# Triangular inverses of large batches on VectorE alone, in row order, with norms from lanes, fix-ups on ScalarE, and a replanned instruction order

## The chip, the cores and the metric

The kernel runs on one core of a Trainium2 chip (TensorE, VectorE, ScalarE, GpSimd, the SyncE DMA queue). The metric is device time in microseconds, the median of the runs: 554.67 us (554.18 to 555.22, three runs).

## What is computed

A delta-rule attention over 768 positions for 16 heads of width 48, followed by two mixture-of-experts layers (8 experts each, top-1). Cut to the part that matters here:

```python
k_n = k / (norm(k) + 1e-06)
for t in range(S):
    y[:, :, t] = q[:, :, t] @ state
    v_old = state^T k_n[:, :, t]
    state = state + beta_t * outer(k_n[:, :, t], v[:, :, t] - v_old)
x = y as [1536, 384]; x = moe(x); out = moe2(x)     # route to argmax expert, relu(x w1) w2, gate
```

## The kernel before

**Tiling.** The 768 positions are cut into 24 chunks of 32. Inside a chunk the recurrence is a triangular system: with the Gram matrix of the chunk's keys, a 32x32 unit triangle is inverted for each of the 16 heads, and the state then moves from chunk to chunk by matrix products. Six groups q of four chunks share their loads.

**Gram matrices.** `gram(q)` multiplies keys with keys and queries on TensorE (L504); ScalarE evicts them to `Gs` (L515) and `PT` (L520); GpSimd masks `PT` (`affine_select`, L550).

**Inverses in lanes.** `inlane(bi, pri)` takes a batch of chunks (`BATCH` = 4, 4, 8, 8 chunks; batches 0 and 1 with `BLK` 1, batches 2 and 3 with `BLK` 0). It writes `Gs` to a DRAM scratch `scrB` (L646), reads it back so that each of 128 lanes (partitions) holds one 32x32 triangle `Bl` (L653), and inverts by substitution on all lanes at once. `c(0)` is the square root of the diagonal on ScalarE (L669); `c(1)` to `c(9)` scale the triangle on VectorE (L671 to L688). The substitution goes over columns kk: `mul` is L711 or L729, `sub` is L715 or L731. Batches 0 and 1 invert only the two 16x16 blocks on the diagonal. Batches 2 and 3 invert the whole triangle. There `parts(kk)` splits the result columns 0 to 9 into two halves with a temporary each (`d["tmp"][:, h]`), both on VectorE, and a second chain does columns 10 and up on GpSimd with `gtmp`; `a0 = (32, 32, 10, 10)[bi]` sets the border. A result `z` goes to a scratch `scrZ` (L771), and `load_zt(c)` brings it into `ztp` (L781), the tile from which TensorE reads the inverse of a chunk.

**Fix-ups.** For chunks 0 to 7 `fix(c)` computes the lower-left block from the two diagonal ones: a transpose on VectorE (`tz`, L796, after the load L792), a product (`f1`, L803), an eviction on ScalarE (`fe`, L807), a second product (`f2`, L814), and four evictions with a sign change into `ztp` on VectorE (`fz`, L818).

**Norms.** `norm(q, h, pair)` computes the norm factors `mt` from the time-major keys: squares on ScalarE (L441), a sum on VectorE (L447), a root on ScalarE (L448), five small VectorE operations (L450 to L454), and a scaling of the values on GpSimd (L465).

**The steps.** `step(c)`, c from 0 to 23, is a loop through one state, one step behind the other: AT (L855, TensorE reads `ztp`), its eviction ATe (L858), U (L867), AS (L872), W evicted in four parts of 32 partitions (`We`, L879), the state update DS (L892) into `Sps`, the state evicted in two halves (`Se`, L900), QS (L886) and PW (L907) for the output, evicted at L919. Two tables say which engine evicts: `WENG, SENG = ("AAAA", "AA") if c < 30 else ("AVAV", "VA")`, so ScalarE does all of them.

**Routing, loads and the rest.** `logits(q)` and `route(g)` rank the tokens of finished groups (L955 to L1049). `load_w` brings the first experts' weights; seven of these loads and three zero fills of `xt2` hang on U of certain steps. The two expert layers come after the attention (`moes`).

**The order.** A class `Plan` holds all instructions of the attention with engine, assumed duration, dependences and priority, and orders them by list scheduling. `LAT` is an assumed latency between engines, `keep_warm` puts dummy matmuls (L840) where TensorE would be idle in the plan. Each engine's and queue's instructions are emitted in that order, and each runs in order; SyncE issues all large DMAs from one queue. On ScalarE and VectorE an instruction that waits holds everything behind it on its engine.

Of the kernel before, what the change touches and what calls it, by code (L numbers as in the profile page):

```python
# [353 lines left out]
def attention(tc, ctx, con, I, C, wg, A, xt1, xa1, xt2, zr, T1, Ti1, place, load_w, late, wts, xb, new_x, gather):  # L354
# [81 lines left out]
    def norm(q, h, pair):  # L436
# [10 lines left out]
        add(k("n2"), "V", 0.06 + 0.2 * n, lambda: nc.vector.tensor_reduce(s0("n2"), T[k("sq")][:, 0:n], axis=AX.X, op=ALU.add), (k("sq"),), uses=(k("sq"),))  # L447
        add(k("s0"), "A", 0.2, lambda: nc.scalar.activation(s0("s0"), T[k("n2")][:, 0:n], AF.Sqrt), (k("n2"),))  # L448
        g = lambda x: T[k(x)][:, 0:n]
        add(k("m0"), "V", 0.08, lambda: nc.vector.tensor_scalar(s0("nt"), g("s0"), 1e-30, None, ALU.max), (k("s0"),))  # L450
        add(k("m1"), "V", 0.17, lambda: nc.vector.reciprocal(s0("nr"), g("nt")), (k("m0"),))
        add(k("m2"), "V", 0.09, lambda: nc.vector.tensor_tensor(g("nr"), g("nr"), g("n2"), ALU.mult), (k("m1"),))
        add(k("m3"), "V", 0.09, lambda: nc.vector.tensor_tensor(g("nr"), g("nr"), g("s0"), ALU.add), (k("m2"),))
        add(k("m4"), "V", 0.08, lambda: nc.vector.tensor_scalar(mt[:, c], g("nr"), 0.5, 1e-6, ALU.mult, ALU.add), (k("m3"),))  # L454
# [37 lines left out]
    def gram(q, pri=0.0):  # L492
# [44 lines left out]
        for hh in range(2):  # L537
            hd = ("G", q, hh)
            f0 = 0 if dbq else starts[b] // 4
            for g in range(2 if dbq else 1):  # L540
                f = q == f0 and hh == 0 and g == 0
                k = (hd, 1 if dbq and g == 0 else 3)
                d0 = ("Ge", 0, 0, 0) if dbq else ("Ge", f0, 0)
                add(("Ge", q, hh, g) if dbq else ("Ge", q, hh), "A", 0.22 if dbq else 0.28, lambda hh=hh, g=g: e1(hh, g), (k,) + (() if f else (d0,)), pri, uses=(hd,) + (() if f else (("Gs", b),)), new=("Gw" if b >= 0 and BLK[b] else "Gs", ("Gs", b)) if f else None)
            add(("Pe", q, hh), "A", 0.3, lambda hh=hh: e2(hh), ((hd, 3),) + ((("Pe", q, 0),) if hh else ()), pri, uses=(hd,) + ((("PT", q),) if hh else ()), new=None if hh else ("PT", ("PT", q)))
# [83 lines left out]
    scrZ = {}  # L629

    def inlane(bi, pri):
# [32 lines left out]
        def c(i):  # L664
            n2 = d["Bl"].rearrange("p i j -> p (i j)")[:, 0:1024:33]
            if i == 0:
                d["tmp"] = sb("ztmp", k("tmp"), [128, 2, 160])
# [10 lines left out]
            elif i < 9 and blk:  # L678
                j = slice(16 * (i - 5), 16 * (i - 5) + 16)
                nc.vector.tensor_tensor(d["Bl"][:, j, j], d["Bl"][:, j, j], d["c"][:, j].unsqueeze(2).to_broadcast([128, 16, 16]), ALU.mult)  # L680
# [11 lines left out]
        for i in (0, 1, 2, 3, 4, 5, 6, 9) if blk else range(10):  # L692
            du = (0.2, 0.11, 0.09, 0.27, 0.11, 0.33, 0.33, 0.33, 0.33, 0.1 * r)[i]
            dp = (prev,) if i else bs
            if i == 4:
# [5 lines left out]

        def sub_blocks(kk):
# [4 lines left out]
            return f(z, kk, gs, 32, 0), f(Bl, 32 * (kk + 1) + kk, 528, 0, 32), f(z, kk + 1, gs, 32, 1), tt  # L707
# [9 lines left out]
        a0 = (32, 32, 10, 10)[bi]  # L717

        def parts(kk):
            J = min(kk // r + 1, a0)  # L720
# [1089 lines left out]
```

## Time and profile before

| | us |
|---|---|
| median of 3 runs | 554.67 |
| span of the profiled execution | 553.6 |
| VectorE busy (share) | 360.8 (65%) |
| TensorE busy | 465.4 (84%) |
| ScalarE busy | 275.1 (50%) |
| GpSimd busy | 187.3 (34%) |

The span is the time from the first to the last instruction of one profiled execution; its own total time isn't recorded, the median stands for it. The page gives busy time and share of each engine, and a view of the span in 40 slices with the granted clock of TensorE. Views of the trace give instructions in order of time, groups by line, the waits with what ended them, and the busy time in chosen stretches. An engine name with a q is its queue, which takes care of waits and of the issue of DMAs.

### The profile page before, as it was taken

The page shows a single profiled execution, that of the slowest core. Times are in us where ns is not written, and L with a number is a line of the kernel's source. Part 1 is how long each engine was busy: PE and PEld are TensorE (multiplying, and loading weights), DVE is VectorE, ACT ScalarE, POOL GpSimd, SP SyncE. Part 2 cuts the span into 40 slices and gives each one's busy share as a digit, 9 for nine tenths or more (in the row PEclk, how much of TensorE's full clock was granted, in tenths as well). Part 3 has the DMA queues.
Part 4 walks back from the last instruction along what each step waited for, and adds up shares of the span by engine and source line. Part 5 has one row for each costly group of instructions (what it writes and reads, how often), then busy time and mean ns, then how long its engine had stood idle before and what let it go on. Part 6 is the DMA issues. An engine that isn't in the chain of part 4 may idle for free. (4 is left out here: it accounts for less than half of the span.)

```text
span 553.6 us, 14924 instructions
## 1 busy us (share of the span) xinstructions
PE 465.4 (84%) x5874; PEld 393.7 (71%) x5885; DVE 360.8 (65%) x1160; ACT 275.1 (50%) x604; POOL 187.3 (34%) x257
## 2 busy tenths in 40 slices
PE   8564877877898859999999999999589999789981
PEld 4232555555665629999999999987469889779860
DVE  8286699999312255787888788898124857366840
ACT  2101345756676744756566575665123845335830
POOL 6454376475100036131451351034503341312111
PEclk9768588979999997999999999999879999999986
DMA  6676756475483231675476395631831590816400
GB/s 181 145 163 102 159 147 138 62 219 126 107 274 96 62 82 45 228 263 193 121 259 242 119 314 154 217 106 52 295 138 40 186 350 20 291 49 239 145 12 14
DMA packets 89733, 85.17 MB, mean 154 GB/s; under 512 B 48735, under 2 KB 71991, under 8 KB 89616
## 3 DMA queue, kind: packets, MB, share of 16 engines
q1 hardware_dynamic: 83872, 71.72, 44.0%
q0 software_dynamic: 5744, 11.95, 7.0%
q8 instruction: 66, 1.08, 0.9%
q14 instruction: 51, 0.42, 0.3%
HBM read 72.52 MB, written 14.86 MB: 158 GB/s over the span
## 5 line engine op out<-in xcount | busy, mean ns | idle before, releaser
L1208 DVE TENSOR_TENSOR l<-r,h 128x768 fp32r<-128x768 f32 x128 | 118.1, 952 | 10.9 <-ACT h L1204 8.0
L1204 ACT ACTIVATE h<-r 128x768 fp32r<-128x768 f32 x128 | 101.8, 837 | 3.1 <-DMA xa<-aux 3.1
L1220 PE MATMUL hp<-xh,h 128*128 128x256 f32 x288 | 84.4, 293 | 7.7 <-DVE fo L1432 3.6
L1220 PE MATMUL y<-h,hh 128*128 128x384 f32 x240 | 84.4, 352 | 0.0
L1222 PE MATMUL hp<-xl,h 128*128 128x256 f32 x288 | 81.8, 284 | 1.0 <-issue 1.0
L1221 PE MATMUL hp<-xh,l 128*128 128x256 f32 x288 | 81.5, 283 | 0.0
L1221 PE MATMUL y<-h,hl 128*128 128x384 f32 x240 | 80.9, 337 | 0.0
L1222 PE MATMUL y<-l,hh 128*128 128x384 f32 x240 | 80.7, 336 | 0.0
L1252 ACT ACTIVATE hh<-hp 128x256 fp32r<-128x256 f32 x96 | 36.3, 383 | 61.9 <-PE hp L1222 51.2
L1255 DVE SCALAR_TENSOR_TENSOR hl<-hp,hh 128x256 fp32r<-128x256 f32 x96 | 39.7, 421 | 38.9 <-ACT hh L1252 26.8
L1220 PEld LDWEIGHTS hp<-xh,h 128*128 128x128 f32 x288 | 55.5, 193 | 9.9 <-issue 7.4
L164 POOL DMA_INDIRECT out<-fo,fix x19 | 22.4, 1181 | 107.0 <-DVE fo L1432 81.3
L1222 PEld LDWEIGHTS hp<-xl,h 128*128 128x128 f32 x288 | 55.5, 193 | 1.3 <-issue 1.2
L1221 PEld LDWEIGHTS hp<-xh,l 128*128 128x128 f32 x288 | 55.9, 194 | 0.1
L164 POOL DMA_INDIRECT xt<-p,rix x16 | 16.7, 1044 | 103.2 <-ACT h L1204 74.0
L1221 PEld LDWEIGHTS y<-h,hl 128*128 128x128 f32 x240 | 45.3, 189 | 0.7 <-issue 0.4
L1220 PEld LDWEIGHTS y<-h,hh 128*128 128x128 f32 x240 | 45.2, 188 | 0.0
L1222 PEld LDWEIGHTS y<-l,hh 128*128 128x128 f32 x240 | 45.1, 188 | 0.0
L206 POOL DMA_INDIRECT xb<-xt,Ti x32 | 36.7, 1146 | 12.7 <-issue 5.8
L879 ACT ACTIVATE wpd<-WA 32x192 f32<-32x192 f32 x96 | 30.8, 320 | 15.8 <-PE WA L872 11.7
L729 DVE TENSOR_TENSOR ztmp<-z,xb 128x100 f32<-128x100 f32 (+30 forms) x118 | 34.9, 331 | 0.6
L1234 ACT ACTIVATE xh<-xp 128x384 fp32r<-128x384 f32 x29 | 14.3, 492 | 42.0 <-PE xp L1231 34.5
(236 smaller groups left out, 901.4 us busy)
## 6 DMA issues: line engine op xcount, KB each, us to landing
r<-moe_w SPq DMA_DIRECT2D x64, 768.0 KB
kq<-kq SPq DMA_DIRECT2D x20, 192.0 KB
xt<-zr SPq DMA_DIRECT2D x3, 776.0 KB
kt<-ktm SPq DMA_DIRECT2D x12, 192.0 KB
vt<-vtm SPq DMA_DIRECT2D x6, 384.0 KB
ztp<-scrZ SPq DMA_DIRECT2D x48, 32.0 KB
xt<-pay SPq DMA_DIRECT2D x16, 96.0 KB
kq<-kq SPq DMA_DIRECT2D x2, 512.0 KB
```

Source lines behind the costliest of these rows:

```text
L164: i = nc.gpsimd.indirect_dma_start(out=dst, out_offset=IO(ap=idx, axis=0), in_=src, in_offset=None, bounds_check=rows - 1, oob_is_err=False)
L206: nc.gpsimd.indirect_dma_start(out=dst, out_offset=None, in_=src, in_offset=IO(ap=ix, axis=0), bounds_check=1536, oob_is_err=False)
L729: ve.tensor_tensor(tt, z[:, a:b, kk : kk + 1].to_broadcast([128, b - a, m]), Bl[:, kk + 1 : 32, kk].unsqueeze(1).to_broadcast([128, b - a, ...
L879: nc.scalar.activation(wp[p, :, Q, :], st["W", c][p], AF.Copy)
L1204: nc.scalar.activation(v(h), v(r), AF.Copy)
L1208: nc.vector.tensor_tensor(v(l), v(r), v(h).bitcast(F32), ALU.subtract)
L1220: nc.tensor.matmul(o, lh, rh, start=first, stop=False)
L1221: nc.tensor.matmul(o, ll, rh, start=False, stop=False)
L1222: nc.tensor.matmul(o, lh, rl, start=False, stop=last)
L1234: nc.scalar.activation(xs()[0][:, :, s], p[0], AF.Copy)
L1252: nc.scalar.activation(hs()[0][:, f], p[0], AF.Relu)
L1255: nc.vector.scalar_tensor_tensor(hs()[1][:, f], p[0], 0.0, hs()[0][:, f].bitcast(F32), ALU.max, ALU.subtract)
```

## The change

It does this:

- Batches 2 and 3: the substitution runs on VectorE only, over all result columns in one operation per product and per difference. The chain on GpSimd, `gtmp`, `a0` and the halves are gone. `ztmp` is one tile of 272 instead of two of 160.
- The triangle is scaled along columns instead of rows (`c` broadcast with `unsqueeze(1)`). The Gram matrix is symmetric, so a product can then read row kk of `Bl`, which is contiguous, in place of column kk, which has a stride of 32 elements. This holds for all four batches.
- Norms of chunks 8 to 23 come from the lanes' diagonal: six small VectorE operations per large batch, `mts(0)` to `mts(5)`, the last a transpose into `mt`. `norm` is called only for q 0 and 1. The scaling of values on GpSimd stays and now waits for `mts(5)`.
- The four `fz` of each chunk 0 to 7 go from VectorE to ScalarE.
- W and state evictions of steps 14 to 23 are split between ScalarE and VectorE (`c < 14` instead of `c < 30`).
- The planner's assumed durations and the VectorE latency are replaced (many small VectorE operations from about 0.08 to about 0.19), so the order is planned anew.

```diff
-    LAT = {("P", "A"): 0.2, ("P", "V"): 0.2, ("V", "V"): 0.1, ("A", "A"): 0.15, ("P", "P"): 0.0, ("S", "S"): 0.0}
+    LAT = {("P", "A"): 0.2, ("P", "V"): 0.2, ("V", "V"): 0.0, ("A", "A"): 0.15, ("P", "P"): 0.0, ("S", "S"): 0.0}
...
-        add(k("m0"), "V", 0.08, lambda: nc.vector.tensor_scalar(s0("nt"), g("s0"), 1e-30, None, ALU.max), (k("s0"),))
+        add(k("m0"), "V", 0.19, lambda: nc.vector.tensor_scalar(s0("nt"), g("s0"), 1e-30, None, ALU.max), (k("s0"),))
...
-                d["tmp"] = sb("ztmp", k("tmp"), [128, 2, 160])
+                d["tmp"] = sb("ztmp", k("tmp"), [128, 1, 272])
...
-                nc.vector.tensor_tensor(d["Bl"][:, j], d["Bl"][:, j], d["c"][:, j].unsqueeze(2).to_broadcast([128, 8, 32]), ALU.mult)
+                nc.vector.tensor_tensor(d["Bl"][:, j], d["Bl"][:, j], d["c"].unsqueeze(1).to_broadcast([128, 8, 32]), ALU.mult)
...
+            if i == 5 and n == 8:
+                dp += (k(("mt", 2)),)
...
+        def mts(i):
+            if i == 0:
+                d["nt"], d["nr"] = [wk.tile([128, 32], F32, name=x, bufs=1) for x in ("lnt", "lnr")]
+                nc.vector.tensor_scalar(d["nt"], d["s0"], 1e-30, None, ALU.max)
+            elif i == 1:
+                nc.vector.reciprocal(d["nr"], d["nt"])
+            elif i == 2:
+                nc.vector.tensor_tensor(d["nr"], d["nr"], d["Bl"].rearrange("p i j -> p (i j)")[:, 0:1024:33], ALU.mult)
+            elif i == 3:
+                nc.vector.tensor_tensor(d["nr"], d["nr"], d["s0"], ALU.add)
+            elif i == 4:
+                nc.vector.tensor_scalar(d["nr"], d["nr"], 0.5, 1e-6, ALU.mult, ALU.add)
+            else:
+                nc.vector.transpose(mt[:, starts[bi] : starts[bi] + 8].rearrange("p c x -> p (c x)"), d["nr"])
+
+        if n == 8:
+            pv = k(("c", 0))
+            for i in range(6):
+                dp = (pv,) + ((k(("mt", 0)),) if i else (("il", bi - 1, ("mt", 5)),) if BATCH[bi - 1] == 8 else ())
+                add(k(("mt", i)), "V", (0.19, 0.36, 0.2, 0.2, 0.2, 0.22)[i], lambda i=i: mts(i), dp, rest(starts[bi]) + 6, uses=(k("Bl"),))
+                pv = k(("mt", i))
+            for cx in range(starts[bi], starts[bi] + 8):
+                add(("v", cx), "G", 0.5, lambda cx=cx: nc.gpsimd.tensor_tensor(T["vt", cx // 4][:, cx % 4 : cx % 4 + 1], T["vt", cx // 4][:, cx % 4 : cx % 4 + 1], mt[:, cx : cx + 1].unsqueeze(3).to_broadcast([128, 1, 4, 48]), ALU.mult), (pv, ("vt", cx // 4)), uses=(("vt", cx // 4),))
...
-        a0 = (32, 32, 10, 10)[bi]
-
         def parts(kk):
-            J = min(kk // r + 1, a0)
-            return [(0, J)] if J < 4 else [(0, J // 2), (J // 2, J)]
+            return [(0, kk // r + 1)]
...
-                    ve.tensor_tensor(tt, z[:, a:b, kk : kk + 1].to_broadcast([128, b - a, m]), Bl[:, kk + 1 : 32, kk].unsqueeze(1).to_broadcast([128, b - a, m]), ALU.mult)
+                    ve.tensor_tensor(tt, z[:, a:b, kk : kk + 1].to_broadcast([128, b - a, m]), Bl[:, kk, kk + 1 : 32].unsqueeze(1).to_broadcast([128, b - a, m]), ALU.mult)
...
-            chains = [("V", "", parts, nc.vector, lambda h: d["tmp"][:, h], prev)]
-            if a0 < M:
-                chains.append(("G", "g", lambda kk: [(a0, kk // r + 1)] if kk // r >= a0 else [], nc.gpsimd, lambda h: d["gtmp"][:, 0], prev))
+            chains = [("V", "", parts, nc.vector, lambda h: d["tmp"][:, 0], prev)]
...
+        FENG = "AAAA"
...
-        def fz(Q):
+        def fz(Q, e):
             r = slice(32 * Q, 32 * Q + 16)
-            nc.vector.tensor_scalar(ztp[(c // 2) % 3][r, ci, :, Q, 16:32], T[F2][r], -1.0, None, ALU.mult)
+            if e == "A":
+                nc.scalar.activation(ztp[(c // 2) % 3][r, ci, :, Q, 16:32], T[F2][r], AF.Copy, scale=-1.0)
+            else:
+                nc.vector.tensor_scalar(ztp[(c // 2) % 3][r, ci, :, Q, 16:32], T[F2][r], -1.0, None, ALU.mult)
...
-        WENG, SENG = ("AAAA", "AA") if c < 30 else ("AVAV", "VA")
+        WENG, SENG = ("AAAA", "AA") if c < 14 else ("AVAV", "VA")
...
     for q in range(NQ):
-        if 4 * q >= NP:
+        if 4 * q >= NP and BATCH[bof(4 * q)] < 8:
             norm(q, 0, False)
```

## Rows read from the trace of the kernel before

**Rows 1.** Busy time by stretch: start:end, length, engines, granted clock, DMA share, GB/s.

```profile
core 0: us, PE busy (x) PEld busy (x) DVE busy (x) ACT busy (x) POOL busy (x), PEclk, DMA share, GB/s
63.60:116.47 52.87, 40.40 (x1297) 29.13 (x1294) 51.26 (x207) 29.16 (x83) 34.24 (x77) 0.88 0.57 127
116.47:148.23 31.76, 26.18 (x613) 18.95 (x613) 26.18 (x124) 20.79 (x59) 15.21 (x32) 0.89 0.54 130
148.23:190.67 42.44, 38.07 (x950) 26.97 (x938) 7.76 (x44) 29.96 (x81) 0.00 (x0) 1.00 0.56 164
```

**Rows 2.** ScalarE in order of time: start, length, line, operation, idle time before and releaser.

```profile
63.60 1.36 ACT L879 ACTIVATE wpd<-WA 32x192 f32<-32x192 f32 x4 [2.48 <-PE WA L867]
...
116.47 1.34 ACT L879 ACTIVATE wpd<-WA 32x192 f32<-32x192 f32 x4
...
144.16 1.35 ACT L879 ACTIVATE wpd<-WA 32x192 f32<-32x192 f32 x4 [0.49 <-PE WA L872]
...
146.53 0.98 ACT L900 ACTIVATE sbd<-Sps 64x384 f32<-64x384 f32 x2
...
148.23 1.36 ACT L879 ACTIVATE wpd<-WA 32x192 f32<-32x192 f32 x4 [0.50 <-PE WA L872]
...
190.67 1.36 ACT L879 ACTIVATE wpd<-WA 32x192 f32<-32x192 f32 x4 [0.36 <-PE WA L872]
```

**Rows 3.** TensorE in order of time, two state updates of neighbouring undisturbed steps.

```profile
145.56 0.86 PE L892 MATMUL Sps<-wpd,kt 128*48 128x192 f32 x8 [0.28 <-ACT wpd L879]
...
149.63 0.86 PE L892 MATMUL Sps<-wpd,kt 128*48 128x192 f32 x8 [0.28 <-ACT wpd L879]
```

**Rows 4.** Waits from 60 to 195 us (us, times, longest), and one root on ScalarE.

```profile
ACT s L448 <- DVE n L447: 11.3, 5, 3.6
...
PE WA L855 <- DVE ztp L818: 8.4, 5, 3.2
...
PE R L1029 <- DVE oh L1019: 1.4, 1, 1.4
...
76.81 0.22 ACT L448 ACTIVATE s<-n 128x16 f32<-128x16 f32 x1 [2.81 <-DVE n L447]
```

**Rows 5.** VectorE in order of time, and GpSimd's scalings as a group (63 to 145).

```profile
33.23 0.28 DVE L711 TENSOR_TENSOR ztmp<-z,xb 128x72 f32<-128x72 f32 x1
33.55 0.23 DVE L715 TENSOR_TENSOR z<-z,ztmp 128x72 f32<-128x72 f32 x1
...
63.40 0.42 DVE L683 TENSOR_TENSOR xb<-xb,lc 128x256 f32<-128x256 f32 x1
...
77.74 0.57 DVE L729 TENSOR_TENSOR ztmp<-z,xb 128x105 f32<-128x105 f32 x2
...
80.95 1.10 DVE L729 TENSOR_TENSOR ztmp<-z,xb 128x95 f32<-128x95 f32 x2
...
L465 POOL TENSOR_TENSOR vt<-vt,mt 128x192 f32<-128x192 f32 x20 | 10.9, 566 | 25.0 <-DVE mt L454 12.5 <-issue 8.3 <-PE Sps L892 4.1
```

**Rows 6.** VectorE's groups from 64 to 99.5 us: busy us, mean ns, idle before.

```profile
L729 DVE TENSOR_TENSOR ztmp<-z,xb 128x60 f32<-128x60 f32 (+30 forms) x59 | 17.6, 334 | 0.3
L731 DVE TENSOR_TENSOR z<-z,ztmp 128x60 f32<-128x60 f32 (+30 forms) x59 | 13.9, 271 | 0.1
L818 DVE TENSOR_SCALAR ztp<-R 16x64 f32<-16x64 f32 x20 | 4.4, 221 | 0.6
```

**Rows 7.** Issues of DMAs on the SyncE queue, and ScalarE's root of batch 2.

```profile
49.43 0.41 SPq L653 DMA_DIRECT2D xb<-scrB  x1
...
55.12 0.26 ACT L669 ACTIVATE ls<-xb 128x32 f32<-128x32 f32 x1 [12.40 <-DMA xb<-scrB]
...
86.20 0.38 SPq L653 DMA_DIRECT2D xb<-scrB  x1
...
99.52 0.38 SPq L771 DMA_DIRECT2D scrZ<-z  x1
104.58 6.65 SPq L781 DMA_DIRECT2D ztp<-scrZ  x12
```

More of the change, by code (lines that the diff above doesn't have):

```diff
@@ L753, in inlane @@
                     m = 31 - kk
-                    if en == "V":
-                        du = sum(0.06 + 0.00104 * (b - a) * m for a, b in cs) + (0.0 if len(cs) > 1 else 0.03)
-                    else:
-                        du = 0.1 + 0.0022 * (cs[0][1] - cs[0][0]) * m
-                    first = en == "G" and kk == a0 * r
-                    def mf(kk=kk, cs=cs, ve=ve, tmp=tmp, first=first):
-                        if first:
-                            gt()
-                        solve(kk, "m", cs, ve, tmp)
-                    us = (k("Bl"), k("z")) + ((k("tmp"),) if en == "V" else () if first else (k("gtmp"),))
-                    add(k((pre + "m", kk)), en, du, mf, (pv,), pri, uses=us, new=("gtmp", k("gtmp")) if first else None)
-                    add(k((pre + "s", kk)), en, du, lambda kk=kk, cs=cs, ve=ve, tmp=tmp: solve(kk, "s", cs, ve, tmp), (k((pre + "m", kk)),), pri, uses=us + ((k("gtmp"),) if first else ()))
+                    du = sum(0.19 + 0.00105 * (b - a) * m for a, b in cs)
+                    us = (k("Bl"), k("z"), k("tmp"))
+                    add(k((pre + "m", kk)), en, du, lambda kk=kk, cs=cs, ve=ve, tmp=tmp: solve(kk, "m", cs, ve, tmp), (pv,), pri, uses=us)
+                    add(k((pre + "s", kk)), en, du, lambda kk=kk, cs=cs, ve=ve, tmp=tmp: solve(kk, "s", cs, ve, tmp), (k((pre + "m", kk)),), pri, uses=us)
                     pv = k((pre + "s", kk))
@@ L940, in step @@
                 wr = (("AS", c - 1), ("QS", c - 1)) if c > 1 else ("sbd%d" % ((c + 1) % 2),)
-                add(("Se", c, hh), e, 0.38 if e == "A" else 0.47, lambda hh=hh, e=e: s_ev(hh, e), (("DS", c),) + wr, r0 - 1.0)
-        add(("PW", c), "P", 0.66, pw_mm, we + (("QS", c),) + tuple(("Pm", q, Q) for Q in range(4)), r0 - 1.5, uses=(("PT", q), O))
-        add(("Oe", c), "A", 0.22, o_ev, (("PW", c),) + ((("Oe", 4 * q),) if i else ()), r0 - 2.0, uses=(O,) + ((("pay", q),) if i else ()), new=("pay", ("pay", q)) if i == 0 else None)
+                add(("Se", c, hh), e, 0.48 if e == "A" else 0.55, lambda hh=hh, e=e: s_ev(hh, e), (("DS", c),) + wr, r0 - 1.0)
+        add(("PW", c), "P", 0.48, pw_mm, we + (("QS", c),) + tuple(("Pm", q, Q) for Q in range(4)), r0 - 1.5, uses=(("PT", q), O))
+        add(("Oe", c), "A", 0.33, o_ev, (("PW", c),) + ((("Oe", 4 * q),) if i else ()), r0 - 2.0, uses=(O,) + ((("pay", q),) if i else ()), new=("pay", ("pay", q)) if i == 0 else None)
     def logits(q):
@@ L1053, in route @@
         f = 0.008 * n
[L1054 to L1056 removed]
+        seq = [("v3", "V", 0.18 + f, v3), ("v4", "V", 0.18 + f, v4), ("v5", "V", 0.18 + f, v5), ("v6", "V", 0.18 + f, v6), ("v7", "V", 0.18 + f, v7)]
+        seq += [(("v8", i), "V", 0.19, lambda i=i: v8(i)) for i in range(n)] + [("rk", "P", 0.35, rk)]
+        seq += [("v12", "V", 0.18 + 2 * f, v12), ("v13", "V", 0.18 + f, v13), ("v14", "V", 0.18 + f, v14)]
         for name, e, du, fn in seq:
@@ L1102, in attention @@
         kd = n > 2
-        add(k, "V", 1.1 if kd else 0.5, lambda t=t: nc.vector.memset(t, 0.0), pri=(300 if kd else 0) - n, after=0.0)
+        add(k, "V", 1.08 if kd else 0.5, lambda t=t: nc.vector.memset(t, 0.0), pri=(300 if kd else 0) - n, after=0.0)
     for c in range(0, NP, 2):
```

57 lines of the change are left out of this document (26 added, 31 removed).

## The prediction, made before the change was run

> **What bounds the kernel now.** I read the share of the engines by stretch first, then the starts of the 24 steps on ScalarE, then who waits for whom, then VectorE's instructions in order of time. The stretches [rows 1] show two kernels in one: behind the steps TensorE is busy nearly without a gap (the experts, by the page's slices); from 63.6 to 190.7 us the 24 attention steps run, and there no engine is full all the time. In the first of their stretches VectorE is (51.26 of 52.87 us), in the last it does next to nothing (7.76 of 42.44). The change touches only what comes before 191 us, so the sum is made over the steps.
>
> A step shows as the eviction of W by ScalarE, L879. The first starts at 63.60, the ninth at 116.47, the fifteenth at 148.23, the last at 190.67 [rows 2]: 8 steps in 52.87 us, 6 in 31.76, 9 in 42.44, 127.07 in all. An undisturbed step takes 4.07 us, from 144.16 to 148.23: W eviction 1.36, TensorE's update of the state 0.86, state eviction 0.98, the rest matmuls of AS and hand-overs [rows 2, 3]. That is a loop through one state, and 23 of them would be 93.6 us. So 33 us of the 127 are disturbance; the question is how much of it the change removes.
>
> The waits [rows 4] name it. TensorE stands 8.4 us at L855 for L818 on VectorE: the fix-up of the next inverse, 0.22 us of work, sits in VectorE's queue among the substitution of batch 2. ScalarE stands 11.3 us (5 times) at the square root L448 for a reduction L447 on VectorE, and W and S evictions are queued behind that root. Only one of the five, 2.81 us at 76.81, belongs to a norm that the change keeps (q=1); 8.5 us go with the other four. Both are queues of steps behind a full VectorE, not work.
>
> **The substitution.** Batch 2 inverts one 32x32 triangle in each lane, column by column. Before, VectorE does result columns 0 to 9 in halves, GpSimd the rest; those GpSimd operations go. VectorE spends 17.6 + 13.9 us on it [rows 6]. After, VectorE does 31 products and 31 differences, (kk+1)(31-kk) elements each for kk from 0 to 30, 5456 per kind. A single dependent difference of 72 elements takes 0.23 us and the 256-element product along rows 0.42 [rows 5], which gives 0.16 + 0.00102 us per element; I add 0.035 to the next start, as from 33.23 + 0.28 to 33.55. So 62 x 0.195 + 10912 x 0.00102 = 12.1 + 11.1 = 23.2 us for a batch. The old product reads a column with a stride, 0.28 for 72 against 0.23 [rows 5], about 0.0008 us per element more at the larger sizes; if the new one still paid it, the batch would be 23.2 + 5456 x 0.0008 = 27.6. I take 23.2, as the 256-element row has the new access pattern. Beside that VectorE loses 20 fix-ups in the batch-2 stretch (4.4 us, [rows 6]), 32 or 7.0 us in all, and four reductions with their small chains; it gains six small operations per large batch, about 1.3 us at the 0.2 of a small operation. Batch 2 now ends at 99.5 (its store is issued at 99.52, [rows 7]). Its input lands at 55.12 [rows 7]; with 4 us of scaling, 23.2 of substitution, 1.4 of the kept norm and transposes each, and 1.3 of new norm it ends near 87.5. That isn't on the path by itself: the store and the loads behind it take about 9 us (99.52 to 104.58 and 4 more, an estimate), so step 8 has its inverse at about 97 and wants it, by the sum below, at about 104.
>
> **The fix-ups on ScalarE.** 32 of them, at 0.22 (VectorE's mean for the same tile, [rows 6]) to 0.34 (a quarter of the 1.36 for 32x192, [rows 2]): 7.0 to 10.9 us in the first 8 steps. I take 0.22, the same tile. They sit in the ScalarE queue between the evictions of W and S, where it waits for TensorE anyway: about 1 us a step in 4.07. Squares and roots of the norms leave it (about 2 us in this stretch). I charge a quarter of 7.0 to the path, 1.9 us with rounding; if nothing hides them, 7.0 to 10.9.
>
> First 8 steps: 52.87 - 8.4 - 4.1 (of the 8.5 of root waits: the longest, 3.6 [rows 4], just ahead of step 8, and 0.5 before) + 1.9 = 42.3 us. What is late next: TensorE, whose granted clock is 0.88 on the mean of this stretch, so not always the upper of its two levels [rows 1], with the last products of keys, and the kept root.
>
> **Steps 8 to 13.** The evictions stay on ScalarE. The other 4.4 us of root waits go: 31.76 - 4.4 = 27.4. I take 27.0, since the routing's short VectorE operations, behind which TensorE stands 1.4 us at L1029 [rows 4], no longer share VectorE with a substitution; six undisturbed steps would be 24.4.
>
> **Steps 14 to 23.** W's four parts and S's two go half to VectorE, which has room there [rows 1]. In the loop W falls from 1.36 to about 0.7 and S from 0.98 to about 0.55 (384 elements by the 0.16 + 0.00102 line, VectorE being the slower half): 1.1 us. TensorE does not allow that much: from state update to state update it runs 4.07 us with 0.28 of waiting shown [rows 3], so its own work is up to 3.79 a step. I take 0.28 off nine steps, 2.5 us. Besides, these nine take 42.44 against 36.6 undisturbed, from routing's evictions and matmuls put between; the loop now has some slack for them, and I take half of the 5.8, 2.9. So 42.44 - 5.4 = 37.0; bounds 42.4 (nothing gained) and 33 (all disturbance gone and 0.12 of gaps in TensorE's 3.79, 3.67 a step).
>
> **The new order, and the rest.** The planner's durations go up to the measured ones (0.08 to 0.19 for a small VectorE operation), so it stops queueing steps behind work that it thinks short; I give that no gain of its own. Nothing is removed before step 0, whose inverse comes through batch 0 and DMA: 63.6 stays, with 1.5 either way. Norms of later chunks now wait for a batch's scratch round trip (input at 55.12, or about 92 for batch 3 if its load, issued at 86.20, takes the 5.7 us that batch 2's took from 49.43, [rows 7]), and GpSimd scales the values from that: both well ahead of steps 8 and 16. The scaling of a batch's triangle now also waits for the product that reads its diagonal (its third new small operation); both are in VectorE's queue, so nothing stands for it. Behind step 23 the routing, the first gather and the experts are as before and move as a block; weight loads are tied to steps and move along.
>
> **Sum.** 42.3 + 27.0 + 37.0 = 106.3 against 127.07: 20.8 us less. The profiled execution has a span of 553.6, 1.1 below the median of 554.67; its own time outside the span isn't shown, so I take that difference for it. 553.6 - 20.8 + 1.1 = 533.9, say 534.0.
>
> **Rivals.** *Substitution becomes the bound.* VectorE alone carries all columns, and if it is late, steps 8 and 16 wait. For it: GpSimd keeps 16 scalings of values for batches 2 and 3 at 0.57 [rows 5] and they slow VectorE. Two 95-element products took 1.10 us while GpSimd computed, two of 105 took 0.57 when it stood still [rows 5]. The Trainium skill, SBUF — State Buffer, "Who interferes with whom", states that a VectorE instruction with two SBUF inputs and a GpSimd instruction reading SBUF exclude each other for a whole instruction; the trace agrees, 0.5 us lost for a GpSimd operation of about that length. Against: most GpSimd work in there was its share of the columns, which goes. Worst case 27.6 + 8 x 0.57 = 32.2 for batch 2, ending near 97 and ready at 106, 2 us late; for batch 3 from about 92 with 4 of scaling, 32.2, 8 of routing between and 9 of store and load, ready at 145 against a want of 63.6 + 42.3 + 27.0 + 7 = 140: 7 us in all, 541.
>
> *The late split gives nothing*, because TensorE in its order is the limit, and a VectorE eviction queues behind routing there: 5.4 back, 539. For it: 3.79 of 4.07 is already TensorE's work. Against: the 42.44 holds 5.8 of disturbance.
>
> *The gain is given back at the experts' start*, if the ten large loads that the code ties to the steps, now within 21 us less, finish late. 0.55 of the DMA engines' time is used in these stretches [rows 1], so 0.66 after: half the gain back at most, 544.
>
> *Slower: ScalarE's queue takes over VectorE's stall.* A fix-up waits for a matmul, that for a transpose on VectorE inside a substitution, that for a DMA. Now the evictions of W and S stand behind it. It costs nothing while the fix-up's input comes within the 1 us or so that a step leaves; every us later is paid in each of 8 steps. From 2.6 us on (8 x 2.6 = 20.8) it eats the whole gain, and at 3.0 the time is 534 + 24 = 558. Against: that transpose is 0.4 us of work and its load comes a pair of chunks ahead; TensorE's wait at L855 (8.4 for 8 steps, 1.05 each) already holds that lateness.
>
> *The change doesn't do what it says*: if the new order leaves the steps where they are, the time stays within 0.2%, 1.1 us, which is about what a measurement here can tell from none.
>
> **How the numbers follow.** Forecast 534 with its own range 527 to 541: 0.66. Substitution the bound, 541: 0.11. Late split without gain, 539: 0.11. Given back, 544: 0.05. No change: 0.03. Slower, 558: 0.04. The bounds of the terms reach further: below, 38.5 (8 x 4.07 and 6 for the products and the clock) + 24.4 + 33 = 95.9 gives 523.5; above, with fix-ups unhidden at 0.22 (40.4 + 7.0), 29 and 42.4, 118.8 gives 546.4. The range is 523.5 to 546.5; it leaves out the last two cases and small tails. Faster by over 0.2%: 0.93, within: 0.03, slower: 0.04.
>
> **What would show it.** Right: step 8 near 106, step 14 near 133, step 23 near 170; no wait at L855 for the fix-up; roots waiting for a reduction only once or twice; one product or difference of 256 elements at 0.40 to 0.45; batch 2's store near 88; late steps under 4.0 us apart with TensorE nearly full. Wrong: step 8 or 16 waiting for loads of the inverse (substitution); late steps still 4.1 or more (split); ScalarE waiting at fix-ups (slower case); the first expert's matmuls waiting for weights (given back).

## The result, and the profile after

The changed kernel takes 539.53 us (median, 538.92 to 543.34), beside 554.42 (553.62 to 555.22) for the kernel before: a ratio of 0.9748, 95% interval 0.9696 to 0.98. That is 15 us less, 5.5 short of the forecast. The profiled execution has a span of 537.2 where before had 553.6. In this document times are medians of all executions, while ratios and their intervals leave out those more than 1.5% above the fastest of their kernel (three of four in e7, one each in e8 and e9).

The stretches of the steps after, as [rows 1] show them of before: microseconds, then busy time of each engine, TensorE's granted clock, share of the DMA engines, GB/s.

```profile
62.89:109.08 46.19, 37.88 (x1292) 28.13 (x1296) 37.22 (x108) 33.00 (x106) 10.12 (x17) 0.96 0.66 151
109.08:135.29 26.21, 24.48 (x635) 17.25 (x623) 17.84 (x66) 19.08 (x52) 3.76 (x8) 1.00 0.70 175
135.29:180.65 45.36, 37.39 (x925) 26.93 (x917) 18.93 (x71) 19.61 (x51) 0.00 (x0) 0.96 0.50 137
```

First 8 steps 52.87 to 46.19, the next six 31.76 to 26.21, and the last nine 42.44 to 45.36: **the late steps became slower**. The steps begin 0.7 earlier, so the 24th starts 10.0 us earlier. The span is 16.4 shorter: 6.4 us more went behind the steps, where the change edits nothing.

The evictions of W in order of time (start, duration, then in brackets the idle time before and who ended it), as [rows 2] of before:

```profile
62.89 0.32 ACT L891 ACTIVATE wpd<-WA 32x192 f32<-32x192 f32 x1
...
109.08 0.32 ACT L891 ACTIVATE wpd<-WA 32x192 f32<-32x192 f32 x1 [0.52 <-PE WA L884]
...
135.29 0.36 DVE L889 COPY wpd<-WA 32x192 f32<-32x192 f32 x1 [4.36 <-ACT ATn L870]
135.68 0.32 ACT L891 ACTIVATE wpd<-WA 32x192 f32<-32x192 f32 x1 [0.49 <-DVE wpd L889]
136.04 0.35 DVE L889 COPY wpd<-WA 32x192 f32<-32x192 f32 x1 [0.39 <-ACT wpd L891]
136.42 0.32 ACT L891 ACTIVATE wpd<-WA 32x192 f32<-32x192 f32 x1 [0.42 <-DVE wpd L889]
...
180.65 0.32 ACT L891 ACTIVATE wpd<-WA 32x192 f32<-32x192 f32 x1 [0.41 <-PE WA L884]
```

From 135.29 on the four pieces do not run side by side. Each starts 0.03 to 0.04 us after the other engine's piece has ended, and all four take 1.45 us where ScalarE alone took 1.36. The waits from 55 to 180 us (total, times, longest), as [rows 4]:

```profile
DVE r L805 <- DMA r<-scrZ: 9.8, 2, 8.2
...
DVE wpd L889 <- ACT wpd L891: 7.7, 8, 3.4
ACT sbd L912 <- DVE sbd L910: 6.9, 5, 1.6
ACT wpd L891 <- DVE wpd L889: 6.1, 10, 0.9
DVE sbd L910 <- ACT sbd L912: 4.4, 3, 1.9
...
DVE nt L450 <- ACT s L448: 2.3, 1, 2.3
```

The two engines wait for each other, for W (`wpd`) and for the state (`sbd`) alike; the first line is used further down. What [rows 4] showed is gone: TensorE's 8.4 us for the fix-up, and ScalarE's 11.3 us for the reduction. VectorE's substitution of batch 2 (64.5 to 93.6 us, groups: busy us, mean ns; the last line is one size from 64 to 94), as [rows 6]:

```profile
L752 DVE TENSOR_TENSOR ztmp<-z,xb 128x87 f32<-128x87 f32 (+15 forms) x29 | 11.2, 388 | 0.9
L754 DVE TENSOR_TENSOR z<-z,ztmp 128x87 f32<-128x87 f32 (+14 forms) x28 | 11.2, 401 | 0.9
...
L752 DVE TENSOR_TENSOR ztmp<-z,xb 128x220 f32<-128x220 f32 x2 | 1.3, 672 | 0.1
```

And batch 2's store and the loads behind it on SP's queue, as [rows 7]:

```profile
93.86 0.38 SPq L778 DMA_DIRECT2D scrZ<-z  x1
...
99.19 6.74 SPq L788 DMA_DIRECT2D ztp<-scrZ  x12
```

New, and foreseen by nobody: groups of matmuls on TensorE broken off in the middle for "issue", that is, with nothing that they wait for in the profile (timeline of TensorE), and the queues of the transfers between 67.4 and 68.4 us:

```profile
69.80 0.36 PE L884 MATMUL WA<-sbd,ATn 128*32 128x96 f32 x3 [1.37 <-issue]
73.95 0.43 PE L812 MATMUL R<-ztp,r 128*32 128x16 f32 x29 [1.53 <-issue]
...
90.93 0.67 PE L879 MATMUL WA<-vt,ztp 128*64 128x48 f32 x15 [1.15 <-issue]
```

```profile
q8 instruction: 1, 0.02, 5.8%
```

From 60 to 107 us they come to 6.5 us, against 0.5 in the same stretch of before. Each ends 1.2 to 1.5 us after a packet of queue q8 (instructions, 16 KB) has landed; the one at 69.80 ends 1.46 us after the packet shown. Behind the steps the same thing (TensorE's waits from 340 to 535 us), before and then after:

```profile
PE hp L1220 <- issue: 10.8, 3, 4.3
PE hp L1222 <- issue: 1.0, 1, 1.0
```

```profile
PE hp L1232 <- issue: 3.9, 1, 3.9
```

That is 7.9 us less of it, in code that the change leaves alone. The granted clock differs there too (0.94 on the mean from 340 us on before, 0.96 after): of the 10.2 us in which it stood at 0.50, the lower of its two levels, from 396.7 on in the kernel before, 3.4 are left after, from 388.5 on, each time within about 1 us of a stall's end. So the 6.4 us are stalls and clock together, and these rows don't part them.

### The profile page after: what moved, and what is told of

Same layout as the page of the kernel before. It is cut to its first block, busy times and chain, and to the rows that moved or that the text cites. A ratio compares the mean times of both kernels' runs of the same rounds, so it can differ in the third digit from the quotient of the medians.

```text
span 537.2 us, 14712 instructions
## 1 busy us (share of the span) xinstructions
PE 460.0 (86%) x5877; PEld 389.4 (72%) x5888; DVE 347.6 (65%) x1033; ACT 267.3 (50%) x599; POOL 150.7 (28%) x173
## 5 line engine op out<-in xcount | busy, mean ns | idle before, releaser
L1232 PEld LDWEIGHTS y<-h,hh 128*128 128x128 f32 x240 | 45.2, 188 | 0.0
L1234 PEld LDWEIGHTS y<-l,hh 128*128 128x128 f32 x240 | 45.1, 188 | 0.0
L1246 ACT ACTIVATE xh<-xp 128x384 fp32r<-128x384 f32 x29 | 14.2, 492 | 40.7 <-PE xp L1243 33.2
L891 ACT ACTIVATE wpd<-WA 32x192 f32<-32x192 f32 x76 | 24.5, 322 | 19.3 <-PE WA L884 11.1
L852 PE MATMUL warm<-const-bfloat16-1.0 128*128 128x512 bf16 x93 | 31.2, 460 | 2.0 <-issue 0.9
```

What stands on the lines that cost most here:

```text
L852: nc.tensor.matmul(t, one_[:, 0:128], one_, start=True, stop=True)
L891: nc.scalar.activation(wp[p, :, Q, :], st["W", c][p], AF.Copy)
L1232: nc.tensor.matmul(o, lh, rh, start=first, stop=False)
L1234: nc.tensor.matmul(o, lh, rl, start=False, stop=last)
L1246: nc.scalar.activation(xs()[0][:, :, s], p[0], AF.Copy)
```

## The experiments

All stages in one table. "First" to "late" are the three stretches above, "behind" goes from the 24th eviction to the end of the span, "fetch" is TensorE's waits for "issue" behind 340 us; all of these from one profiled execution (for e4 the slowest of its nine, 561.7 us, for e7 one of 547.86), the time is the median of 4 to 10 runs (one run for e12). e9 and e10 are the programs of the changed kernel and of e1, run again: first, late and fetch differ between two executions of one program by up to 1.4, 0.1 and 3.8 us.

| kernel | us | first 8 | 8 to 13 | late 9 | behind | fetch |
|---|---|---|---|---|---|---|
| before | 554.4 | 52.9 | 31.8 | 42.4 | 362.9 | 11.8 |
| changed | 539.5 | 46.2 | 26.2 | 45.4 | 356.6 | 3.9 |
| e9, changed again | 539.2 | 45.5 | 26.1 | 45.5 | 359.1 | 7.7 |
| e1, no late split | 531.6 | 43.7 | 26.5 | 40.1 | 355.8 | 8.5 |
| e10, no late split again | 534.0 | 45.1 | 26.4 | 40.2 | 357.5 | 9.5 |
| e2, pieces side by side | 533.3 | 44.2 | 26.5 | 40.7 | 356.1 | 8.0 |
| e11, side by side from step 8 | 553.8 | 44.4 | 28.1 | 47.9 | 367.3 | 13.3 |
| e3, before, blocks shifted | 551.4 | 53.0 | 33.6 | 43.0 | 354.0 | 4.8 |
| e4, new plan only | 556.5 | 53.5 | 37.7 | 41.8 | 365.4 | 10.4 |
| e5, substitution and plan | 546.6 | 53.2 | 26.6 | 45.5 | 357.8 | 6.6 |
| e6, e1 with the old norms | 536.0 | 44.0 | 26.0 | 42.3 | 359.7 | 10.3 |
| e7, e1 with fix-ups on VectorE | 547.9 | 49.8 | 24.6 | 45.2 | 362.7 | 10.5 |
| e8, e1 with the old plan | 549.7 | 48.9 | 25.6 | 45.0 | 362.6 | 12.2 |
| e12, e1, blocks shifted | 548.7 | 47.2 | 25.6 | 42.2 | 367.1 | 14.7 |

**The late split.** Three kernels: without it (e1, e10), with its pieces side by side (e2), and the changed kernel again on the same chip as e10 (e9).

```
-        WENG, SENG = ("AAAA", "AA") if c < 14 else ("AVAV", "VA")
+        WENG, SENG = ("AAAA", "AA") if c < 30 else ("AVAV", "VA")
```

> The changed kernel, but steps 14 to 23 evict on ScalarE alone again, as they did before the change. Theory (the split pieces run in strict turns, one engine waiting for the other at every piece, so that a first eviction takes 1.45 us where ScalarE alone took 1.36, and a state eviction 1.07 against 0.99): the nine steps from 14 to 23 take 42.4 us or less instead of 45.4, and the kernel 536 to 537 us. Rival (the stage is longer because the new order puts the routing's work between the steps, and the split costs nothing): the nine steps stay at 45 us and the kernel at 539.5. The number of TensorE instructions ahead of the experts' branch differs by a few, so up to 4.3 us may come or go behind the steps; the steps themselves decide.

```profile
62.56:106.23 43.67, 36.13 (x1292) 26.96 (x1292) 37.28 (x108) 32.86 (x106) 10.21 (x17) 1.00 0.68 152
106.23:132.71 26.48, 24.45 (x634) 17.31 (x623) 18.13 (x66) 18.94 (x53) 3.75 (x8) 1.00 0.71 187
132.71:172.77 40.06, 36.72 (x930) 25.79 (x919) 7.80 (x44) 29.31 (x78) 0.00 (x0) 1.00 0.56 155
```

Those are e1's stretches. 531.61 us (530.32 to 534.38), ratio to before 0.9655 (0.9606 to 0.9705): the late steps are 5.3 us shorter without the split. They are 2.4 shorter than in the kernel before as well, so the new order and the emptier queues help there, and the split, with the order planned for it, did the harm.

> The changed kernel itself once more, on one chip with the two kernels below. Theory (the split in turns costs the changed kernel some 5 us in the steps from 14 on): these nine steps take 44.5 us or more again, and the kernel is 5 to 9 us behind the one with the late steps' evictions in place or side by side. Rival (what separated them was the clock's fall at 149.6 us and the chip's day): the nine steps take 42 us or less where the clock is not halved in them, and the kernels are within 2 us.

> The changed kernel with the late evictions on ScalarE alone once more (531.6 us before), beside the changed kernel on one chip. Theory (turns): 5 to 9 us faster than the changed kernel, the nine steps at 40 to 42 us. Rival (clock and chip): within 2 us of it.

539.19 us (534.62 to 543.1; ratio 0.9695, 0.9633 to 0.9757) against 533.97 (533.09 to 535.54; 0.9651, 0.9612 to 0.9689). The intervals to before overlap, so the time alone would not settle it; the stretch does: 45.50 against 40.18 with a granted clock of 1.00 in both. So it is the split and not the clock. The turns themselves make an eviction of W 0.1 and one of the state 0.08 to 0.14 us longer in most steps, an estimated 2 us in nine; the rest of the 5.3 lies in steps with routing (step 16 comes 6.06 us after step 15 in e9, 4.68 in e10), where the order was planned for evictions side by side. How it divides is not shown.

For e2 the framework is told that pieces on different engines don't depend on each other; as they lie in different partitions, nothing else is needed:

```
+            if "V" in WENG:
+                apart([f"We{c}_{min(Q, R)}{max(Q, R)}" for R in ((1, 3) if Q % 2 == 0 else (0, 2))], i)
...
+            if "V" in SENG:
+                apart([f"Se{c}"], i)
```

where `apart` declares instruction `i` free of dependence within each group.

> The changed kernel, but with the waits between ScalarE's and VectorE's pieces of one eviction taken out (the pieces lie in different partitions), so that the two halves run side by side. Theory (the turns are what the split lost; the halves as such are worth what was predicted): a first eviction takes 0.7 us instead of 1.45 and a state eviction 0.55 instead of 1.07, the nine steps from 14 to 23 come to 37 to 39 us, and the kernel to 531 to 533. Rival (TensorE's own work and its waits for instructions set these steps): the nine steps stay at 41 to 42.5 us, the same as with ScalarE alone, and the kernel comes to 536 to 537.

```profile
132.37 0.67 ACT L896 ACTIVATE wpd<-WA 32x192 f32<-32x192 f32 x2
132.38 0.73 DVE L894 COPY wpd<-WA 32x192 f32<-32x192 f32 x2 [4.20 <-ACT ATn L875]
...
135.57 0.67 ACT L896 ACTIVATE wpd<-WA 32x192 f32<-32x192 f32 x2
...
163.76 0.52 PE L905 MATMUL O<-sbd,kq 128*32 128x96 f32 x11 [1.80 <-issue]
```

Now the halves start 0.01 us apart, an eviction takes 0.74 us, and the step from 132.37 to 135.57 takes 3.20. So neither the reading of one PSUM tile by two engines nor TensorE stands against it: the turns come from the dependences that the framework adds. TensorE's order here is that of the changed kernel, so the 4.7 us by which the stretch is shorter are the turns', with that order. Yet the stretch is 40.66, between theory and rival, and the kernel takes 533.26 us (0.9688, 0.9633 to 0.9743), no less than e1. The first seven of the nine steps take 28.85 us (e1: 31.89); the next takes 8.61, with the stall at 163.76 and a granted clock of 0.60 from 163.7 to 168. The gain is there and is lost again in one place, in this one profile.

e11 puts the split at step 8 (`c < 8`), pieces side by side.

> The kernel with the two engines' pieces side by side, and with the split from step 8 on instead of step 14. Theory (TensorE's own work is the limit of an undisturbed step: 24.5 of 26.5 us in the six steps from 8 to 14 with ScalarE alone): these six steps come to 25 to 26.5 us, the nine behind them to 37 to 41, the kernel to 529 to 533, no clear gain over ScalarE alone. Rival (the loop through one state is the limit, and 1.1 us of it goes with each split step): the six steps take 21 us or less, the kernel 525 or less.

Both missed. In e11, batch 3's store on SP's queue, TensorE ahead of step 16, two evictions, and the busy time of the undisturbed step from 150.25 to 153.58; then, from the kernel before, a line of TensorE between the two rows of [rows 3]:

```profile
137.29 0.38 SPq L778 DMA_DIRECT2D scrZ<-z  x1
...
146.12 0.95 PE L1021 MATMUL R<-cst,lgs 128*128 128x8 f32 x8
146.92 0.81 PE L852 MATMUL warm<-const-bfloat16-1.0 128*128 128x512 bf16 x3
147.67 1.08 PE L872 MATMUL WA<-ztp,kt 128*48 128x128 f32 x16
...
153.58 0.67 ACT L896 ACTIVATE wpd<-WA 32x192 f32<-32x192 f32 x2
...
156.84 0.32 ACT L896 ACTIVATE wpd<-WA 32x192 f32<-32x192 f32 x1 [0.58 <-PE WA L889]
...
150.25:153.58 3.33, 3.25 (x105) 2.47 (x96) 2.58 (x10) 1.84 (x5) 0.00 (x0) 1.00 0.55 119
```

```profile
148.93 0.42 PE L955 MATMUL R<-cst,r 128*96 128x128 f32 x2
```

An undisturbed step takes 3.26 us, or 3.33 with a whole step's matmuls in it; of these 3.33 TensorE is busy 3.25. So TensorE is the limit there, but its own work is 3.25 and not 3.79: the 3.79 had 0.42 of the routing's transposes (L955) in it. Step 16 comes 9.65 us after the one before. Routing (L1021) and dummy matmuls (L852) stand in TensorE's queue ahead of the matmuls that open it (L872, at 147.67), but they only fill the time: these matmuls wait for batch 3's inverse, whose loads are issued from 143.72 on and have landed at 147.04 by their semaphores. Its store is at 137.29, in e2 at 127.66: VectorE's evictions of steps 8 to 13 stand among batch 3's substitution. Two later steps take 8.1 and 8.3. With 10.7 us more behind the steps than the changed kernel has, the ratio is 0.998 (0.9945 to 1.0014): all gain gone.

**The parts of the first steps.** e4 is the kernel before with the planner's new numbers alone (the new durations and latency of the diff, but for those of operations that it doesn't have). Its substitution keeps its old durations, and these are too short: a pair of products of 105 elements is planned at 0.34 us and takes 0.57 [rows 5].

> The kernel before with the planner's new durations and latency alone: the order of all queues is planned anew, no operation changes but for their order (the substitution keeps its halves, its strided rows and GpSimd's share, the norms and the fix-ups stay where they were). Theory (the gain of the first 14 steps comes from work taken off VectorE and from the fix-ups' place, not from the order): 551 to 556 us, the first 14 steps 82 to 85 us as before (84.6), with VectorE's fix-ups still waited for by TensorE. Rival (the old durations were too short, so the old order queued the fix-ups behind substitution; right durations alone cure that): the first 14 steps come to 75 us or less, and the kernel to 546 us or less.

```profile
PE WA L856 <- DVE ztp L819: 5.8, 3, 2.5
...
ACT s L449 <- DVE n L448: 6.7, 2, 4.2
```

Those are its waits from 61 to 150 us: both old queues are still there. 556.5 us, 1.0072 (1.0027 to 1.0117). Alone the plan makes it slightly slower; the rival falls. The theory's 82 to 85 us for the first 14 steps was missed too: 91.2, in the slowest of nine executions.

> The kernel before with two parts of the change: the substitution on VectorE alone, in single operations along rows, and the planner's new durations (which without it gave nothing). Norms come from the keys as before, the fix-ups stay on VectorE, no late split. Theory (VectorE's work in the substitution is what everything else queues behind: batch 2's stretch held 31.5 us of it where single operations take 23, so the roots and the fix-ups wait less too): the first 14 steps fall from 84.6 us to 75 to 78, the kernel to 541 to 546. Rival (the queueing is what costs, and it is cured only by moving the roots and the fix-ups off the queue): the first 14 steps stay above 81 us, the kernel at 550 or more.

546.62 us (0.9834, 0.9769 to 0.99), just above the theory; but the first 14 steps take 79.8 us, between the two, and of them step 8 alone 11.3. Its cause shows in the next runs, which are e1 with one part put back: e7 the fix-ups' place, e8 the planner's old numbers, e6 the norms. The edit of e7:

```
-        FENG = "AAAA"
+        FENG = "VVVV"
```

> The changed kernel without the late split (531.6 us), with the 32 fix-ups on VectorE again, each planned at the same 0.23 us. Theory (the prediction's term: TensorE waits for a fix-up in VectorE's queue among the substitution, 8.4 us in the kernel before, against 1.9 of ScalarE's time on the path): 4 to 8 us come back in the first 8 steps, 43.7 to 48 us or more, the kernel 536 to 539, with TensorE's wait for the fix-up there again at 3 us or more. Rival (planned at their true duration the fix-ups find room between the products, and off ScalarE's queue they delay no eviction): the first 8 steps take 44.5 us or less and the kernel 529 to 532.

> The changed kernel without the late split (531.6 us), with the planner's old durations and latency for all but the substitution's new operations and the fix-ups. All parts of the change but the new numbers are in. Theory (the durations as such are worth nothing, as the prediction took it, and as they gave nothing to the kernel before): 530 to 534 us. Rival (the parts pay only with an order planned on true durations): 538 us or more, with queues of steps behind VectorE in the first 14 steps.

Batch 2's store on SP's queue and the first matmuls of step 8 on TensorE, in e7 and then in e8:

```profile
100.35 0.38 SPq L778 DMA_DIRECT2D scrZ<-z  x1
...
111.15 1.08 PE L867 MATMUL WA<-ztp,kt 128*48 128x128 f32 x16
```

```profile
99.14 0.38 SPq L777 DMA_DIRECT2D scrZ<-z  x1
...
108.02 0.35 SPq L426 DMA_DIRECT2D kt<-ktm  x1
...
113.50 1.08 PE L866 MATMUL WA<-ztp,kt 128*48 128x128 f32 x16
```

e7: 547.88 us, the median of 536.93, 547.86, 547.90 and 551.93; the trace is of the 547.86. It has no ratio, and the lowest time lies where its theory put it, so e7 alone settles nothing. e8: 549.65 (0.9897, 0.9833 to 0.9961), where its rival was. In neither does TensorE wait for a fix-up as it did. Steps 0 to 7 take about as long as in e1 and the changed kernel (39.7 and 38.7 us against 38.4 and 41.0; e8 begins them 4.4 us later than e1), but step 8 comes 10.1 and 10.2 us after step 7, where e1 needs 5.2: batch 2 is stored at 99 to 100, its loads are issued at 106.3 and 108.5, and step 8 has its inverse late. In e8 some 3 us of that are SP's queue: a load of keys (L426) stands ahead of these loads and is held until 108.02 by a state update, though the store has landed at 104.90. In e5 the store is at 99.71, and TensorE stands 0.8 us for the loads just before step 8. In e1 it is at 91.56, in the changed kernel at 93.86.

e5 and e6 differ in nothing but the place of the fix-ups, on VectorE in e5 and on ScalarE in e6, and ran on one chip: 546.62 against 535.98 us (541.17 to 547.47, 529.85 to 537.37), the first 8 steps 53.2 against 44.0, step 8 11.3 against 4.3 us after step 7, batch 2's store at 99.71 against 92.62. So the place of the fix-ups is worth some 10 us here, mostly through batch 2, and the planner's durations are needed beside it (e8). That single operations are needed too is not shown: no run leaves them out and keeps the rest. Parts don't add up: against the kernel before on the same chip, 8 us are left in e5 and 5 in e8 (7 in e7 by its median, 18 by its lowest), of 20 to 21 in e1 and e10.

Batch 3 has such a deadline as well. Where its store is at 132.8 to 140.6 (e6, e12, e11, e5, e8; e7 at 133.8 with 5.6), step 16 comes 7.4 to 10.1 us after step 15; in e1, e2 and e10, at 127.7 to 129.4, it is 4.4 to 4.8. That is probably much of what these runs lose in the late steps; the trace was followed for e11 alone.

For e6 the lanes' norms are removed from e1 (`mts` and what calls it) and all chunks' norms come from the keys.

> The changed kernel without the late split (531.6 us in the run before), with the norms of the chunks from 8 on taken from the keys again: four squares and roots on ScalarE, four reductions and chains on VectorE return, the norms from the lanes go. Theory (the prediction's term: an eviction queues behind a root that waits for VectorE, 8.5 us in the kernel before): 4 to 9 us come back, 536 to 540 us, and ScalarE waits again for the reductions, 3 us or more in all, within the first 14 steps. Rival (with VectorE relieved the reductions are done in time, so the roots cost nothing): within 2 us of 531.6, the roots not waiting.

```profile
DVE n L447 <- ACT sq L441: 4.9, 1, 4.9
```

535.98 us (529.85 to 537.37), 0.9642 (0.9573 to 0.9711): not to be told from e1, whose ratio is 0.9655, though outside the rival's 2 us. ScalarE's roots wait for no reduction; of the pair, the reverse is left, VectorE waiting for a square. The norms are worth little once VectorE has room, at most some 4 us.

**Waits for instructions.** e3 adds three matmuls of 16 columns, whose output nobody reads, at the start of the kernel before; e12 adds 64 to e1:

```
+    t_ = ps.tile([128, 512], F32, name="warm")
+    for _ in range(64):
+        nc.tensor.matmul(t_[:, 0:16], one_[:, 0:128], one_[:, 0:16], start=True, stop=True)
```

> The changed kernel with the late evictions on ScalarE alone, and 64 matmuls of 16 columns (128 instructions of TensorE with their weight loads) more at its start, whose output nobody reads. Theory (TensorE's stalls in the first eight steps fall on the boundaries of blocks of 256 of its instructions, which are fetched by transfers of 16 KB): the stalls of 0.5 to 1.3 us move back by 128 instructions, so that they stand in other groups of matmuls: none at the old places (matmuls of AS of steps 1 and 2, the fix-up's matmuls near 71, PW near 79, U near 88, QS near 92 us), new ones in the first product of a fix-up near 69.6 and in PW near 73.9 and 90 in that kernel's times, each ending 1.2 to 1.8 us after a fetch has landed; their sum stays at 3 to 7 us. Rival (the stalls belong to these instructions and to what they wait for): they stay in the old places.

TensorE's timeline, e1 and then e12:

```profile
68.60 0.36 PE L884 MATMUL WA<-sbd,ATn 128*32 128x96 f32 x3 [1.23 <-issue]
72.48 0.43 PE L812 MATMUL R<-ztp,r 128*32 128x16 f32 x29 [1.26 <-issue]
76.03 0.28 PE L884 MATMUL WA<-sbd,ATn 128*32 128x96 f32 x3 [0.49 <-issue]
```

```profile
69.94 0.54 PE L504 MATMUL R<-kq 64*32 64x64 f32 x35 [1.33 <-issue]
74.46 0.64 PE L812 MATMUL R<-ztp,r 128*32 128x16 f32 x52 [2.03 <-issue]
78.83 0.28 PE L919 MATMUL O<-wpd,PT 128*32 128x48 f32 x5 [1.54 <-issue]
```

The stalls leave their old places and stand half a block earlier, each of the first six 63 or 64 matmuls (dummies left out), also at the three places that the theory named: the first in products of keys (L504) instead of AS of step 1, the second in the first group of the fix-up's products (L812, 52 of its 64 left) instead of behind it, the third in PW of step 1 (L919) instead of AS of step 2. In e1 they come after 2220, 2473, 2728 and 2984 recorded matmuls and weight loads, one about every 255; a packet of 16 KB goes with each. Their sum in e12's first steps is 6.9 us. The whole, one execution: 548.7 us, because behind the steps the waits grew from 8.5 to 14.7, one of them 8.2 long.

> The kernel before, with three matmuls of 16 columns more at its very start, whose output nobody reads. That gives TensorE's program ahead of the experts' branch as many instructions as it has in the changed kernel; nothing else differs. Theory (some 4.3 us of the gain behind the steps is nothing that the change does: TensorE waits for its own instructions behind that branch, twice or once, as the blocks in which they are fetched happen to fall): the stall of 4.3 us near 400 us is gone, the steps start within 0.3 us of where they were, and the kernel takes 549 to 551 us. Rival (the time behind the steps came from the change's work, by transfers or by the clock): 554 to 555 us, with both stalls.

```profile
PE hp L1223 <- issue: 4.1, 1, 4.1
PE hp L1225 <- issue: 0.7, 1, 0.7
```

Those are e3's waits from 340 us on: 4.8 where the kernel before has 11.8, and the second stall near 400 is gone. What lies behind the steps shrank from 362.9 to 354.0. But the steps did not stand still: they begin 1.1 us later and take 129.6 instead of 127.1, and the measured time is 551.4 (0.9984, 0.9952 to 1.0016), 1.4 less and not 4.3. That a shift of six instructions goes with other stalls there is what one profile of each shows; the price in the median is not shown, and two executions of the changed kernel's program differ by 3.8 us of stalls as well (3.9 and 7.7).

## Why the prediction was right, and where not

**The sum.** The forecast was 534.0, 523.5 to 546.5; 539.5 lies inside, 5.5 above. But it isn't the same sum: the steps gave 10.0 us instead of 20.8, and 6.4 came from behind them, where the prediction had put nothing. Of the three stretches the first came 3.9 us longer than forecast, the second 0.8 shorter, the third 8.4 longer. Terms that were too hopeful and an unforeseen gain partly covered each other, so that the time lies within the range is in part luck.

**The late split** is the step that failed: -5.4 was taken, +2.9 came, and against e1 the split itself is +5.3. The loop would lose 1.1 us of eviction only if both engines read one PSUM tile at the same time, and that they may was taken for granted; the trace of before has no such pair, and the bound named for this term, 42.4, "nothing gained", should have gone above. The second half of the argument, TensorE's 3.79 us of own work as a floor, was right in kind and too high: it is 3.25 in e11, and steps of 3.20 and 3.26 ran whose AT stood in a neighbouring step. Summing an engine's busy time within a step that waits on a loop counts work (here 0.42 of routing, or AT) that can move out of it. The rival "late split gives nothing" named the right place with a wrong cause.

**The first 8 steps**: 42.3 predicted, 46.2 measured, 43.7 to 45.5 in three more profiles of that order (e1, e9, e10). TensorE's waits for instructions there, 4.9 to 6.6 us, are a term that was missing, though how much of them is on the path is not shown. In the kernel before they come to 0.5 us; that they were hidden beneath its other waits there is an argument that no run tests. In the changed kernel the granted clock was 0.96 too: the step from 70.25 to 79.08 took 8.83 us at 0.81 (8.83 in e9 at 0.61), where e1 and e10 at 1.00 need 7.45 and 7.50.

**Substitution.** 23.2 us for a batch with gaps; the two groups above are busy 22.4 for 57 of the 62 operations, with 1.8 idle between, so about 25 in all. An operation of 255 elements takes 0.42, as taken from 256 in [rows 5]; the strided price is gone. The 2 us too many are GpSimd's: eight operations that ran beside it lie 2.4 us in all above the prediction's line of 0.16 + 0.00102 per element, and the other 54 lie on it within 0.04 each. The two products of 220 elements, 672 ns on the mean, took 0.77 beside its masking of PT and 0.57 beside its scaling of values, where one alone takes 0.39 (at 103.50 in e1). That is the interference that the prediction named, smaller than its rival's price, and 1.7 of the 2.4 come from the masking, which it didn't count. A masking of 0.71 to 0.74 us cost VectorE 0.38 to 0.52, a scaling of 0.59 to 0.67 cost it 0.19: less than the whole instruction of the rule that the prediction cites. The 0.5 us that it read off the kernel before for one GpSimd operation were lost beside two, of 0.47 and 0.42 us. Batch 2's store was put near 88 and came at 93.86. The parts of the predicted end add up to 86.4, not 87.5. The largest piece that was left out stands ahead of the substitution: batch 2's root starts at 54.51, but VectorE begins the scaling only at 58.90, because the transpose of a fix-up (L805) stands ahead of it in its queue and waits 8.2 us for its load (the first of the waits above). In the kernel before, VectorE stood 3.6 us for that load (until 59.22). Then come 2.3 in which the kept norm waits for its root and 1.6 for the next load. That the end "isn't on the path by itself" was too sure: with the store at 99 to 100 (e5, e7, e8) step 8 comes 5 to 6 us late, with the store at 97.11 (e12) it doesn't. The rival "substitution becomes the bound" is what happens then.

**The fix-ups**: right in place (no wait of TensorE for them), half right in cause. What they did on VectorE, once planned right, was not to keep TensorE waiting (0.5 us in e5) but to make batch 2 late (e5 against e6). On ScalarE they cost next to nothing: it waited for a fix-up's matmul 0.7 us in all, so the rival in which its queue takes over the stall didn't come.

**Norms from lanes**: 8.5 us of root waits were to go with them. They went, and stayed away when the norms came back (e6). So the waits were the full VectorE's, not the norms'.

**Steps 8 to 13**: 27.0 predicted, 26.2 measured. Right.

**The new order** was given nothing. Alone that is right (e4, slightly slower); with the other parts it is worth some 15 us (e8 is 5 below its kernel before, e1 and e10 are 20 to 21; some 3 of it is the key load in SP's queue). A zero given to a part by itself is no zero for the sum.

**The start of the experts**: nothing was given back; no wait of the first expert's matmuls for a weight load shows.

## What to carry to other kernels

When an eviction is split over two engines, look in the trace for the first pair: if each piece starts as the other ends, suspect the framework's order on the tile, which could be lifted here, where the pieces share no data. Parts that relieve one queue are not additive: ask which deadline the queue has to keep (here the stores of batches 2 and 3, near 94 and 130 us), and count a part by whether the deadline is kept without it. And before a few microseconds far from the edit are put down to it, look at what waits for nothing there.

## What the runs showed of the hardware

TensorE waits for its own instructions. In stretches of small matmuls, where a block of 255 matmuls and weight loads lasts about 4 us, each block's end costs up to 2.0 us in the first steps (2.8 in a late one of e11); the stall ends 1.2 to 1.7 us after the 16 KB packet of queue q8 has landed. Behind 340 us, in the experts' code, single stalls reach 3.7 to 8.2 us, and over fourteen profiles with the same expert code they come to between 3.9 and 14.7 us, with 354.0 to 367.3 us behind the steps; the five profiles above 10.4 of them are all above 362, though one with 10.4 has 365.4. The Trainium skill, Runtime: NRT & Kernel Launch, "Instruction fetch mechanics", states that each engine fetches blocks of 16 KB, 256 instructions, by a queue of its own while it runs the one before, and that crossing a block's end is mostly hidden. The size agrees; hidden it was not. A handful of instructions more or less ahead of that code may therefore move what lies behind the steps by several microseconds, whatever they do; e3 and e12 fit that, with one profile each. Executions of one program differ there too: the two of the changed kernel's program have 3.9 and 7.7 us of these stalls and 356.6 and 359.1 us behind the steps.

What stays open: how much of the stalls in the first steps is on the path, and why the clock falls to its lower level in those steps in some executions of one order and not in others.
